# Casting v in its load, state casts and stores on GpSimd, and a new order of steps in an RWKV-5 kernel with a ReLU-squared MLP

## The chip, the cores and the metric

The kernel runs on one core of a Trainium2 chip. The metric is device time in microseconds of one launch, taken as the median of several runs. Engines are named as in the profile: PE is TensorE (PEld its weight loads), DVE is VectorE, ACT is ScalarE, POOL is GpSimd, SP is SyncE. ACTq, POOLq and SPq are the same engines when they issue transfers.

## The reference

For each of 4 batches and 8 heads, with head size 48 and 768 steps, a linear recurrence runs over time; its output, rearranged to 3072 rows of 384, goes through two matrices with a squared ReLU between them.

```python
for t in range(S):
    cur = einsum('bhd,bhe->bhde', u[None] * kt, vt)
    y[:, :, t] = einsum('bhd,bhde->bhe', rt, state + cur)
    state = w[None, :, :, None] * state + einsum('bhd,bhe->bhde', kt, vt)
x = y.transpose(0, 2, 1, 3).reshape(B * S, H * D)
g = maximum(x @ w_in, 0) ** 2          # 384 -> 2048
out = g @ w_out                        # 2048 -> 384
```

All inputs and the output are float32; the kernel multiplies in bf16.

## The kernel before, in words

The time axis is cut into 6 chunks of 128 steps. A *unit* is one chunk of one batch: 24 units, unit i being chunk i // 4 of batch i % 4. For each unit, r and k are loaded and scaled by powers of w (`scale`), turned so that the head dimension lies on the partitions, multiplied (`at`), masked (`mask`), and multiplied with v (`y`), with the state carried from the chunk before; the state is kept in float32 (`st32`) and cast to bf16 (`stb`). The result `yb` is turned (`xT`) and goes through the MLP: `m1` (four pieces for a unit alone, eight for a pair), `relu`, a square on ACT (`sqA`) or DVE (`sqD`), `m2` in four quarters, the eviction `osb` and the store `out`. Units 0 to 5 are handled singly and turned on TensorE; from unit 6 on they go in pairs and are turned by transposing transfers.

Nothing is scheduled by rule: the string `ORDER` names every step, in order, with the PSUM bank it uses behind an `@`, and every engine executes its instructions in that order. A word is step.unit.part. Those that the text below speaks of:

- `kt.i.o`, `rt.i.o`: load half o of k or r of unit i, 96 KB, on SP (line L281); for later units both units of a pair come in one load of 384 KB (L278). `ktA.1.0` is such a half, issued by ACT. `vt.i`: load v on POOL. `I.q`, `O.q`: load quarter q of `w_in` or `w_out` on POOL, cast to bf16 by the load (L288, L291).
- `w.0`, `w.1`: powers of w, an activation each on ACT (L242), from `lnat.0` and `lnat.1` on DVE; `wk`, `wr`: two more on ACT (L245). `scale.i.0` scales r with `w.0`, `scale.i.1` scales k with `w.1`, both on DVE (L303).
- `turn.i.x` turns scaled r (x=0) or k (x=1) on TensorE (L333), `rkT.i.x` evicts it on ACT (L337); `kb.i` and `kbT.i` turn k back. `rk.i` multiplies r and k on DVE (L360), `at.i`, `mask.i.o` (L377), `d.i`, `dv.i`, `y.i`, `yb.i` (L456), `xturn.i`, `xT.i` (L481) lead to the MLP.
- `cols`, `copied`, `uwb`, `end`, `wend`: columns of w and u, turned on TensorE, copied on DVE (`copied`), made into the operands of `d` on POOL (`uwb`), the decay over a chunk on ACT (`end`) and spread out on POOL (`wend`, L268), which the first `sadd` needs.
- `fill.n` are n matmuls of a constant tile (L216) whose result is never read.

Every transfer signals a semaphore. Those issued by SP and ACT share eight (DMAHW0 to 7) and those by POOL another eight (DMASW0 to 7), given out in turn when the program is built. A transfer adds 16 to its semaphore when it has landed, and the engine that issues it first waits until the transfer before it on the same semaphore has landed.

Of the kernel before, what the change touches and what calls it, by code (L numbers as in the profile page):

```python
# [21 lines left out]
scale.2.0 at.1@67 kbT.1 kt.5.0 d.1@3 scale.2.1 m1.0.0@2 vt.5 mask.1.0 rt.5.0 s.1@4 turn.2.0@5 relu.0.0 mask.1.1 O.0
turn.2.1@1 rkT.2.0 fill.2 m1.0.3@6 sadd.1 O.3 rt.5.1 sqA.0.0 dv.1 y.1@0 relu.0.3 scale.3.0 O.1 rt.6 yb.1 stb.1
turn.3.0@2 rkT.2.1 scale.4.0 xturn.1@7 rkT.3.0 sqD.0.3 kt.5.1 kb.2@5 xT.1 at.2@43 rk.2 O.2 kbT.2 turn.4.0@6 mask.2.0
m1.1.2@0 rkT.4.0 kt.6 scale.3.1 d.2@1 vb.3 s.2@2 m1.1.0@7 mask.2.1 relu.1.2 sadd.2 turn.3.1@5 sqA.1.2 m1.0.2@4 dv.2
rkT.3.1 y.2@6 m1.1.3@3 relu.1.0 rk.3 yb.2 relu.0.2 kb.3@0 m1.0.1@2 scale.4.1 sqA.1.0 xturn.2@1 kbT.3 m1.1.1@5
relu.0.1 s.3@7 xT.2 d.3@6 sqD.0.1 at.3@40 relu.1.1 turn.4.1@2 mask.3.1 m1.2.2@1 vb.4 rkT.4.1 dv.3 m1.2.3@5 relu.2.2
mask.3.0 at.4@02 vb.5 rk.4 m2.0.0@6 relu.2.3 mask.4.0 sqA.2.2 m1.2.1@1 sqD.2.3 relu.1.3 m1.2.0@4 mask.4.1 sqA.0.2
sqD.1.3 m2.1.0@5 stb.2 relu.2.0 sadd.3 kb.4@0 y.3@3 relu.2.1 sqD.1.1 y.4@2 stb.3 m2.0.1 yb.3 kbT.4 scale.5.0 m2.1.1
sqA.2.0 sqD.2.1 kt.8 xturn.3@4 s.4@7 xT.3 turn.5.0@1 sadd.4 m2.1.2 rkT.5.0 dv.4 m1.3.1@3 sdec.4 kt.10 yb.4 m1.3.0@0  # L30
stb.4 relu.3.1 scale.6.0 m2.0.2 scale.5.1 relu.3.0 xturn.4@4 scale.7.0 m2.0.3 sqA.3.0 rt.8 sqD.3.1 xT.4 m1.3.3@1
osb.0 scale.6.1 turn.5.1@7 out.0 relu.3.3 m1.4.0@2 scale.7.1 rkT.5.1 m2.3.0@3 sqD.3.3 relu.4.0 rkD.6 m1.4.3@0 rk.5
sqA.4.0 kb.5@4 relu.4.3 at.5@61 m1.4.2@7 kbT.5 mask.5.0 vtS.6 m1.4.1@2 sqD.4.3 relu.4.2 mask.5.1 m2.3.1 sqA.4.2
s.5@0 relu.4.1 y.5@4 dv.5 m2.1.3 sqA.4.1 vtS.8 sadd.5 m1.3.2@6 yb.5 osb.1 sdec.5 out.1 relu.3.2 m2.2.0@7 scale.8.0
stb.5 scale.8.1 m2.2.1 rt.10 sqA.3.2 scale.9.0 m2.2.2 scale.9.1 m2.2.3 m2.3.2 osb.2 rkD.8 rk.6 at.6@1205 xturn.5@4
mask.7.1 m2.4.0@6 xT.5 out.2 mask.6.1 m2.4.1 vb.6 mask.7.0 rt.12 m1.5.3@7 mask.6.0 s.6@5 relu.5.3 s.7@4 dv.6 y.7@2
y.6@0 dv.7 m2.4.2 sqD.5.3 vtS.10 vb.8 m1.5.0@1 yb.6 yb.7 m2.4.3 relu.5.0 sadd.7 xD.6 m1.5.1@7 scale.10.0 sqA.5.0
scale.10.1 m2.3.3 osb.4 relu.5.1 sdec.7 out.4 m1.5.2@0 scale.11.1 osb.3 stb.7 m2.5.0@2 scale.11.0 sqA.5.1 sadd.6
out.3 at.8@1467 relu.5.2 rk.8 rkD.10 m2.5.1 sqA.5.2 mask.8.0 s.8@3 mask.8.1 s.9@5 kt.12 m2.5.2 sdec.6 y.8@0 sadd.8
stb.6 m2.5.3 scale.12.0 mask.9.0 osb.5 sadd.9 out.5 mask.9.1 kt.14 vb.10 m1.6.0@1 sdec.9 dv.8 m1.6.4@4 relu.6.0  # L40
scale.13.0 m1.6.3@2 yb.8 vtS.12 sqA.6.0 sdec.8 m1.6.6@6 relu.6.4 dv.9 relu.6.3 m1.6.7@7 sqA.6.4 sqD.6.3 m1.6.1@3
relu.6.7 rk.10 rt.14 y.9@1 relu.6.6 m1.6.2@0 sqD.6.7 stb.9 relu.6.1 yb.9 at.10@4527 relu.6.2 scale.12.1 s.11@6 xD.8
m1.6.5@3 sqA.6.1 mask.11.1 sqA.6.2 s.10@1 dv.11 m2.6.0@0 vtS.14 relu.6.5 dv.10 m2.6.1 scale.13.1 sqA.6.6 mask.10.0
sqA.6.5 m2.7.0@7 stb.8 rkD.12 mask.11.0 m2.7.1 mask.10.1 m2.7.2 sadd.10 vb.12 m2.6.2 sadd.11 kt.16 sdec.10 m2.6.3
sdec.11 y.10@3 osb.6 y.11@4 stb.10 yb.10 out.6 m2.7.3 stb.11 yb.11 m1.8.0@2 scale.14.0 osb.7 xD.10 scale.14.1
m1.8.1@5 relu.8.0 scale.15.0 m1.8.7@1 scale.15.1 sqA.8.0 out.7 m1.8.3@6 relu.8.1 kt.18 relu.8.7 m1.8.2@0 sqA.8.1
kt.20 sqD.8.7 m1.8.6@3 relu.8.2 m2.8.0@4 relu.8.3 sqA.8.2 m1.8.4@7 sqD.8.3 relu.8.6 at.12@2510 rk.12 relu.8.4 m2.8.1
mask.13.1 sqA.8.6 rkD.14 s.12@6 mask.12.0 sqA.8.4 m1.8.5@3 vb.14 mask.12.1 s.13@7 m1.10.5@0 relu.8.5 sadd.12 rt.16
sadd.13 y.12@2 sqA.8.5 sdec.12 m1.10.6@5 relu.10.5 sdec.13 m2.8.2 stb.12 mask.13.0 sqA.10.5 m1.10.3@3 vtS.16 dv.13
relu.10.6 m1.10.0@0 dv.12 relu.10.3 yb.12 m1.10.1@1 sqA.10.6 sqD.10.3 relu.10.0 y.13@7 vtS.18 m1.10.7@5 relu.10.1  # L50
yb.13 sqA.10.0 m2.8.3 xD.12 relu.10.7 m1.10.4@6 osb.8 sqD.10.7 stb.13 m1.10.2@3 out.8 rk.14 relu.10.4 at.14@2017
vtS.20 relu.10.2 m2.9.0@5 sqA.10.4 mask.14.0 sqA.10.2 s.15@4 mask.15.1 m2.9.1 sqA.10.1 dv.15 rt.18 m2.9.2 sadd.15
m2.11.0@6 mask.15.0 vb.16 sdec.15 m2.11.1 scale.16.0 m2.11.2 scale.16.1 rt.20 m2.11.3 scale.17.0 mask.14.1 s.14@3
osb.11 y.15@2 dv.14 m2.9.3 vb.18 out.11 sadd.14 rt.22 stb.15 y.14@7 scale.17.1 osb.9 m1.12.0@4 sdec.14 out.9
m1.12.7@1 yb.14 stb.14 yb.15 relu.12.0 m1.12.3@0 relu.12.7 rkD.16 m1.12.2@6 sqA.12.0 sqD.12.7 m1.12.1@3 relu.12.3
xD.14 relu.12.2 m1.12.4@5 sqD.12.3 relu.12.1 scale.18.0 m1.12.6@7 sqA.12.2 scale.18.1 m1.12.5@2 sqA.12.1 scale.19.0
m2.10.0@4 relu.12.4 vtS.22 scale.19.1 relu.12.5 scale.20.0 m2.13.0@1 sqA.12.4 scale.20.1 m2.10.1 scale.21.0 sqA.12.5
m2.13.1 scale.21.1 vb.20 rkD.18 m2.10.2 relu.12.6 m2.10.3 sqA.12.6 scale.22.0 m2.13.2 osb.10 scale.23.0 rkD.20
m2.13.3 m2.12.0@0 osb.13 m2.12.1 rk.16 out.13 out.10 at.16@6352 kt.22 s.16@7 mask.17.0 m1.14.5@4 sadd.16 m1.14.1@1
relu.14.5 dv.16 s.17@5 vb.22 mask.16.0 m2.12.2 dv.17 relu.14.1 m1.14.2@4 sadd.17 sqA.14.5 m1.14.7@7 mask.16.1  # L60
sqA.14.1 sdec.17 m1.14.0@6 relu.14.2 sdec.16 relu.14.7 y.16@1 rk.18 sqA.14.2 m1.14.4@5 yb.16 relu.14.0 m2.12.3
sqD.14.7 relu.14.4 m1.14.6@3 osb.12 mask.17.1 sqA.14.4 m1.14.3@4 out.12 rk.20 sqA.14.0 y.17@7 relu.14.3 at.18@1650
yb.17 stb.17 m2.15.0@2 sqD.14.3 xD.16 relu.14.6 mask.18.0 s.21@4 stb.16 m2.14.0@7 sqA.14.6 dv.21 m2.15.1 mask.18.1
s.18@3 mask.19.0 m2.15.2 sadd.18 m2.15.3 dv.18 y.18@1 osb.15 sdec.18 m2.14.1 yb.18 out.15 stb.18 m2.14.2 scale.22.1
mask.19.1 m2.14.3 scale.23.1 s.20@4 s.19@6 osb.14 dv.20 at.20@5321 rkD.22 dv.19 y.19@0 mask.20.0 m1.16.0@7 mask.21.1
out.14 m1.16.2@4 relu.16.0 yb.19 m1.16.1@5 sqA.16.0 mask.21.0 xD.18 m1.16.5@1 relu.16.2 mask.20.1 relu.16.1
m1.16.3@7 sadd.19 relu.16.5 y.21@0 sdec.19 sqA.16.1 m1.16.7@2 stb.19 y.20@4 relu.16.3 m2.16.0@3 yb.20 sqA.16.2
m1.16.6@5 sqD.16.3 relu.16.7 sqA.16.5 yb.21 m1.16.4@6 sqD.16.7 relu.16.6 xD.20 m2.17.0@1 relu.16.4 rk.22 m2.17.1
sqA.16.6 at.22@7420 sqA.16.4 s.22@5 m1.18.4@6 mask.23.0 mask.23.1 m2.17.2 relu.18.4 dv.22 m1.18.6@2 sqA.18.4
mask.22.0 y.23@0 relu.18.6 mask.22.1 m1.18.7@6 sqA.18.6 s.23@5 m1.18.1@7 dv.23 relu.18.7 m1.18.3@2 sqD.18.7  # L70
relu.18.1 m1.18.2@4 sqA.18.1 m1.18.5@5 relu.18.3 relu.18.2 y.22@6 sqD.18.3 m1.18.0@7 relu.18.5 yb.22 sqA.18.2
m2.16.1 yb.23 sqA.18.5 m2.16.2 xD.22 relu.18.0 m2.16.3 sqA.18.0 m2.17.3 osb.16 m1.20.0@2 out.16 osb.17 m2.19.0@4
out.17 relu.20.0 m2.19.1 sqA.20.0 m1.20.4@5 m1.20.7@6 relu.20.4 m2.18.0@0 sqA.20.4 m1.20.1@7 relu.20.7 m1.20.6@3
sqD.20.7 relu.20.1 m2.18.1 sqA.20.1 m2.19.2 relu.20.6 m1.22.2@1 sqA.20.6 m2.19.3 relu.22.2 m1.22.1@2 sqA.22.2
m1.20.2@5 osb.19 relu.22.1 out.19 m1.22.4@6 relu.20.2 m2.20.0@7 sqA.22.1 sqA.20.2 m1.20.3@3 relu.22.4 m2.18.2
# [547 lines left out]
```

## Time and profile before

| | |
|---|---|
| median of 3 runs | 174.9 us (174.62 to 177.03) |
| profiled execution, its time | 173.95 us |
| profiled execution, its span | 172.2 us |
| TensorE clock granted in the profile | 1.00 |
| busy: PE / DVE / ACT / POOL | 165.0 / 121.9 / 131.4 / 15.9 us |
| `fill` matmuls | 104, 10.3 us |
| transfers | 28.86 MB, mean 168 GB/s |

The span is the time between the first and the last event of the program on the core, as the profiler recorded it; the execution's own time is 1.75 us more. Rows of the views in order of time give the start and the length of a run of equal instructions, in microseconds, then engine, line, operation, tiles and count. Rows that group instructions give busy time and the mean of one in nanoseconds, then the idle time just before them and what ended it. Rows of transfers give the issuing engine, the count, the size and the median time from issue to landing.

### The profile page before, as it was taken

The numbers are of one execution on the slowest core, as the hardware profiler recorded it, in microseconds if no ns is written. First come the engines' busy times: TensorE is split into PE (matmuls) and PEld (weight loads), VectorE is DVE, ScalarE is ACT, GpSimd is POOL, SyncE is SP. The second block draws the span as 40 slices with busy tenths as digits, with TensorE's granted clock in tenths as the row PEclk, the third lists the DMA queues.
The fourth block names the chain that finished last, engine by engine and source line by source line (L and its number), as shares of the span: only waits on it lengthen the run. The fifth ranks groups of instructions, "written<-read, shape, count | busy, mean of one in ns | idle before, by whom it ended". The sixth has DMA issues, their size and how long they took to land.

```text
span 172.2 us, 4759 instructions
## 1 busy us (share of the span) xinstructions
PE 165.0 (96%) x1964; PEld 135.8 (79%) x1964; DVE 121.9 (71%) x243; ACT 131.4 (76%) x255; POOL 15.9 (9%) x36
## 2 busy tenths in 40 slices
...
GB/s 95 180 289 235 277 235 216 209 197 243 154 247 222 247 194 236 203 173 251 168 227 230 186 201 245 165 239 212 46 213 50 0 25 116 0 46 49 0 127 58
DMA packets 91493, 28.86 MB, mean 168 GB/s; under 512 B 82864, under 2 KB 90672, under 8 KB 91472
## 3 DMA queue, kind: packets, MB, share of 16 engines
...
q0 software_dynamic: 2624, 4.33, 12.4%
q10 hardware_dynamic: 432, 0.25, 0.6%
...
q14 instruction: 6, 0.05, 0.1%
...
## 4 chain that ended last, share of the span: by engine, by line
PE 81%; DMA 8%; DVE 4%; ACT 2%; SPq 2%; issue 1%; DVEq 0%
PE bank L517 34%; PE bank L493 31%; DMA rkT<-rkw 5%; DMA rt<-in_r_dram 4%; PE bank L369 3%; PE bank L441 2%; PE bank L398 2%; PE bank L447 2%; SPq L281 2%; PE bank L533 2%; PE bank L410 1%; PE bank L333 1%; PE bank L216 1%; DVE rkw L303 1%; DVE am L377 1%
## 5 line engine op out<-in xcount | busy, mean ns | idle before, releaser
L493 PE MATMUL bank<-xT,w_in_q 128*128 128x256 bf16 (+1 forms) x720 | 72.1, 251 | 0.0
L517 PE MATMUL bank<-w_out_q,g 128*128 128x384 bf16 x368 | 67.6, 326 | 0.0
L493 PEld LDWEIGHTS <-w_in_q 128*128 128x128 bf16 x720 | 64.0, 113 | 3.3
L501 ACT ACTIVATE gr<-bank 128x512 f32<-128x512 f32 x96 | 55.1, 603 | 10.0 <-PE bank L493 9.8
L517 PEld LDWEIGHTS <-g 128*128 128x128 bf16 x368 | 34.3, 98 | 18.3
L508 ACT ACTIVATE g<-gr 128x512 bf16<-128x512 f32 x68 | 42.0, 640 | 0.8
L510 DVE TENSOR_TENSOR g<-gr 128x512 bf16<-128x512 f32 x28 | 19.3, 688 | 24.1 <-ACT gr L501 23.9
L377 DVE TENSOR_TENSOR am<-bank,smask 128x512 bf16<-128x512 f32 x48 | 31.5, 683 | 3.8 <-PE bank L369 3.7
L524 ACT COPY osb<-bank 128x384 f32<-128x384 f32 x23 | 11.0, 479 | 10.7 <-PE bank L517 10.6
L456 DVE TENSOR_TENSOR yb<-bank,dv 128x384 bf16<-128x384 f32 x24 | 12.9, 551 | 1.0 <-PE bank L447 0.8
L420 DVE TENSOR_TENSOR dv<-vb,bank 128x384 f32<-128x384 bf16 x24 | 12.8, 547 | 0.9 <-PE bank L398 0.5
L432 ACT CAST stb<-st 128x384 bf16<-128x384 f32 x20 | 10.4, 523 | 3.1 <-DVE st L428 3.0
L216 PE MATMUL bank<-warm 128*128 128x128 bf16 x104 | 10.3, 269 | 1.1 <-DVE warm L161 1.1
L301 DVE TENSOR_TENSOR rkw<-rt,wpos 128x384 bf16<-128x384 f32 x18 | 9.8, 551 | 0.8 <-DMA rt<-in_r_dram 0.8
L316 ACT CAST vb<-vt 128x768 bf16<-128x768 f32 x9 | 7.6, 841 | 3.4 <-DMA vt<-in_v_dram 3.4
L301 DVE TENSOR_TENSOR rkw<-kt,wneg 128x384 bf16<-128x384 f32 x18 | 9.8, 550 | 0.0
L216 PEld LDWEIGHTS <-warm 128*128 128x128 bf16 x104 | 8.7, 124 | 1.2 <-DVE warm L161 1.0
L369 PE MATMUL bank<-rkT 64*128 64x128 bf16 x192 | 8.0, 219 | 0.9 <-DMA rkT<-rkw 0.9
L424 DVE TENSOR_TENSOR st<-bank,st 128x384 f32<-128x384 f32 x16 | 8.6, 550 | 0.2 <-PE bank L398 0.2
L441 PE MATMUL bank<-vb,am 128*128 128x48 bf16 x192 | 8.7, 183 | 0.0
L357 DVE TENSOR_TENSOR rk<-rkT 128x1024 bf16<-128x1024 bf16 x9 | 6.2, 686 | 3.4 <-DMA rkT<-rkw 3.4
L428 DVE TENSOR_TENSOR st<-st,wend 128x384 f32<-128x384 f32 x16 | 8.6, 551 | 0.0
...
## 6 DMA issues: line engine op xcount, KB each, us to landing
...
rt<-in_r_dram SPq DMA_DIRECT2D x9, 384.0 KB, 4.8
kt<-in_k_dram SPq DMA_DIRECT2D x9, 384.0 KB, 4.8
vt<-in_v_dram SPq DMA_DIRECT2D x9, 384.0 KB, 5.3
w_in_q<-in_moe_w_in_dram POOLq DMA_DIRECT2D x4, 384.0 KB, 8.2
w_out_q<-in_moe_w_out_dram POOLq DMA_DIRECT2D x4, 384.0 KB, 13.0
...
kt<-in_k_dram SPq DMA_DIRECT2D x11, 96.0 KB, 7.6
```

Source lines behind the costliest of these rows:

```text
L216: nc.tensor.matmul(out=banks[0][:, :128], lhsT=warm, rhs=warm, start=True, stop=True)
L301: nc.vector.tensor_tensor(t["rkw"][:, x, :, :, :D], pair(src), pair(wneg if x else wpos), ALU.mult)
L369: nc.tensor.matmul(out=t["at"][o][:, p, :], lhsT=t["rkT"][sl, 1, p, :], rhs=t["rkT"][sl, 0, p, :], start=True, stop=True,)
L377: nc.vector.tensor_tensor(am, t["at"][o], smask.unsqueeze(1).to_broadcast([C, HP, C]), ALU.mult)
L420: nc.vector.tensor_tensor(t["dv"], t["vb"], t["d"].unsqueeze(2).to_broadcast([C, H, D]), ALU.mult)
L441: nc.tensor.matmul(out=y[:, 2 * p + o, :], lhsT=t[f"am{o}"][:, p, :], rhs=t["vb"][:, 2 * p + o, :], start=(o == 0 and p == 0), stop=c == 0 ...
L456: nc.vector.tensor_tensor(t["yb"], t["y"], t["dv"].rearrange("p h d -> p (h d)"), ALU.add)
L493: nc.tensor.matmul(out=t["h", s][:, a], lhsT=turned, rhs=chunks[c]["xT"][:, b : b + m, n, :], start=(n == 0), stop=(n == NK - 1),)
L501: nc.scalar.activation(t["gr", s], t["h", s], AF.Relu)
L508: nc.scalar.activation(g, x, AF.Square)
L510: nc.vector.tensor_tensor(g, x, x, ALU.mult)
L517: nc.tensor.matmul(out=t["o"], lhsT=chunks[units[i][0]]["g"][:, f, units[i][1], :], rhs=w_out_q[f // 4][:, f % 4, :], start=(f == 0), stop ...
```

## The change

- v of units 0 to 5 is loaded by POOL straight into the bf16 tile `vb`; the cast on ACT (`vb.0` to `vb.5`) goes.
- The first state cast of each batch (`stbP.0` to `stbP.3`) is a copy on POOL instead of ACT.
- The stores of units 0 to 21 (`outP`) are issued by POOL instead of SP; those of units 22 and 23 stay on SP.
- The string `ORDER` is another one: order, banks and the number of fills (57 in place of 104).

```diff
 ORDER = """
-kt.0.0 kt.0.1 rt.0.0 rt.1.0 I.0 rt.1.1 ids fill.25 log@4567 ktA.1.0 lnat.0 rt.2.0 vt.0 lnat.1 w.0 fill.1 cols@1
-kt.1.1 w.1 upper copied kt.2.0 end scale.0.0 wk kt.2.1 vt.1 scale.0.1 wr fill.14 turn.0.0@2 rt.2.1 turn.0.1@3 zeros
-rkT.0.0 rt.3.0 vt.2 rkT.0.1 scale.1.0 rt.3.1 uwb fill.16 at.0@14 rk.0 kb.0@5 mask.0.1 turn.1.0@6 I.3 kbT.0 rt.4.0
-mask.0.0 fill.4 d.0@7 rkT.1.0 I.2 vb.0 vb.1 rt.4.1 dv.0 wend fill.17 s.0@2 y.0@3 scale.1.1 kt.3.0 vb.2 vt.3 yb.0
...
-sqD.22.3 m2.20.3 m1.22.6@0 osb.20 m2.21.3 out.20 relu.22.6 m2.22.0@1 sqA.22.6 m2.22.1 osb.21 out.21 m2.22.2 m2.22.3
-m2.23.0@4 osb.22 out.22 m2.23.1@5 osb.23.0 out.23.0 osb.23.1 out.23.1
+rt.0.0 kt.0.0 kt.0.1 rt.1.0 I.3 rt.1.1 ids lnat.0 fill.17 log@4567 kt.1.1 vt.0 w.0 lnat.1 cols@3 ktA.1.0 rt.2.0
+scale.0.0 upper w.1 rt.2.1 fill.3 turn.0.0@2 vt.1 scale.0.1 kt.2.0 rkT.0.0 copied kt.2.1 wk I.0 fill.5 turn.0.1@2 wr
+I.2 rt.3.0 rkT.0.1 vt.2 rk.0 fill.6 at.0@16 scale.1.0 rt.3.1 kb.0@7 zeros mask.0.0 turn.1.0@2 uwb kt.3.0 mask.0.1
+rkT.1.0 kbT.0 scale.1.1 fill.10 y.0@3 d.0@2 kt.3.1 turn.1.1@7 dv.0 s.0@4 rkT.1.1 rt.4.0 yb.0 end rk.1 fill.8 kb.1@1
+rt.4.1 wend xturn.0@5 at.1@76 scale.2.0 xT.0 kbT.1 rt.5.0 mask.1.0 I.1 fill.7 turn.2.0@3 mask.1.1 d.1@2 rkT.2.0 O.0
+fill.1 m1.0.0@7 kt.4.0 scale.2.1 vt.3 sadd.0 y.1@5 turn.2.1@1 dv.1 kt.4.1 rkT.2.1 stbP.0 yb.1 relu.0.0 m1.0.3@2 vt.4
+rk.2 rt.5.1 scale.3.0 at.2@31 relu.0.3 kb.2@4 O.1 mask.2.1 kt.5.0 xturn.1@5 d.2@7 kbT.2 m1.0.2@0 xT.1 dv.2
+turn.3.0@6 kt.5.1 relu.0.2 mask.2.0 m1.1.3@4 sqA.0.0 scale.3.1 y.2@3 rkT.3.0 m1.1.0@1 rt.6 yb.2 turn.3.1@5 relu.1.0
+s.1@7 kt.6 xturn.2@3 s.2@0 sadd.1 rkT.3.1 m1.1.2@6 sadd.2 stbP.1 relu.1.3 m1.0.1@2 scale.4.0 O.3 relu.1.2 sqD.0.3
...
+sqA.22.5 relu.22.0 m1.22.3@0 relu.22.7 m2.19.3 sqA.22.2 m2.21.1 sqA.22.0 m2.21.2 relu.22.3 osb.19 sqD.22.3 m2.22.0@3
+outP.19 sqD.22.7 m2.21.3 m2.20.2 osb.21 m2.20.3 m2.22.1 osb.20 m2.22.2 outP.20 outP.16 m2.23.0@4 outP.18 outP.21
+outP.17 m2.22.3 m2.23.1@2 osb.23.1 osb.22 osb.23.0 out.22 out.23.1 out.23.0
 """
...
     def load_v(i):
         c, b = units[i]
-        whole = of_two("vt", i, loads, [C, H, D], F32)
         if i >= NH:
+            whole = of_two("vt", i, loads, [C, H, D], F32)
             nc.sync.dma_start(out=whole.rearrange("s b h d -> s (b h) d"), in_=both(v, i))
         else:
-            nc.gpsimd.dma_start(out=tiles[i]["vt"], in_=v[b, :, c * C : (c + 1) * C, :].rearrange("h s d -> s h d"))
+            of_two("vb", i, work, [C, H, D])
+            nc.gpsimd.dma_start(out=tiles[i]["vb"], in_=v[b, :, c * C : (c + 1) * C, :].rearrange("h s d -> s h d"))
...
-    def state_cast(i):
+    def state_cast(i, copy=nc.scalar.copy):
         b = units[i][1]
-        nc.scalar.copy(stb[b], st32[b])
+        copy(stb[b], st32[b])
...
-    def store(i):
+    def store(i, queue=nc.sync):
         c, b = units[i]
-        nc.sync.dma_start(out=out[b * S + c * C : b * S + (c + 1) * C, :], in_=tiles[i]["osb"])
+        queue.dma_start(out=out[b * S + c * C : b * S + (c + 1) * C, :], in_=tiles[i]["osb"])
```

The first instructions of ScalarE in the two built programs, with the semaphores that they wait for and the count (W), and the semaphore of each load (U):

```
before                                        changed
load wrow            U DMAHW0                 load wrow            U DMAHW0
load rt.0.1          U DMAHW2                 load rt.0.1          U DMAHW2
lnw                  W DMAHW0 16              lnw                  W DMAHW0 16
load ktA.1.0         U DMAHW7                 w.0                  W DVE 17
w.0                  W DVE 17                 load ktA.1.0         W DMAHW1 48, U DMAHW1
w.1                  W DVE 18                 w.1                  W DVE 18
```

In the changed program the loads on DMAHW1 ahead of `ktA.1.0` are `rt.0.0`, `rt.2.1` and `rt.4.1`, SP's 1st, 8th and 16th; `rt.2.1` waits for `rt.0.0`, and `rt.4.1` for `rt.2.1`. On POOL, in both, the loads of each semaphore follow each other in the order of the list.

More of the change, by code (lines that the diff above doesn't have):

```diff
@@ L22 @@
[L22 to L75, printed above, removed]
-relu.20.3 m2.18.3 sqA.22.4 sqD.20.3 m1.20.5@1 osb.18 m1.22.5@4 out.18 relu.20.5 m2.21.0@2 sqA.20.5 m2.21.1 relu.22.5
@@ new lines @@
+turn.3.0@6 kt.5.1 relu.0.2 mask.2.0 m1.1.3@4 sqA.0.0 scale.3.1 y.2@3 rkT.3.0 m1.1.0@1 rt.6 yb.2 turn.3.1@5 relu.1.0
+s.1@7 kt.6 xturn.2@3 s.2@0 sadd.1 rkT.3.1 m1.1.2@6 sadd.2 stbP.1 relu.1.3 m1.0.1@2 scale.4.0 O.3 relu.1.2 sqD.0.3
+kb.3@7 xT.2 at.3@01 O.2 sqA.0.2 rk.3 turn.4.0@4 mask.3.0 m1.1.1@3 sqA.1.0 mask.3.1 d.3@6 kbT.3 m1.2.1@5 relu.1.1
+scale.4.1 y.3@0 rkT.4.0 dv.3 m1.2.3@7 relu.2.1 yb.3 turn.4.1@1 relu.0.1 m1.2.0@4 sqD.1.3 rkT.4.1 m2.1.0@3 scale.5.0
+relu.2.3 sqD.1.1 m1.2.2@2 relu.2.0 sqD.0.1 at.4@75 kb.4@6 mask.4.0 turn.5.0@4 kbT.4 s.3@1 m2.0.0@0 mask.4.1 rkT.5.0
@@ new lines @@
+xturn.3@6 rk.4 m2.1.1 xT.3 sqD.2.1 sqA.1.2 s.4@5 y.4@7 dv.4 relu.2.2 m2.0.1 rt.8 sadd.3 m1.3.1@4 scale.5.1 stbP.3
+sadd.4 m2.1.2 stbP.2 relu.3.1 yb.4 vt.5 m1.3.3@1 vtS.6 sqA.2.0 scale.6.0 turn.5.1@5 m1.3.0@7 rkT.5.1 scale.7.0
+xturn.4@2 m2.0.2 xT.4 sqA.2.2 m2.0.3 scale.6.1 kt.8 relu.3.0 m2.1.3 scale.7.1 sqD.2.3 at.5@75 osb.1 kb.5@4 mask.5.1
+m1.4.0@2 kbT.5 rkD.6 rk.5 relu.3.3 m2.2.0@6 mask.5.0 relu.4.0 m2.2.1 sqD.3.3 s.5@2 scale.8.0 m1.3.2@1 sadd.5 rt.10
+m1.4.3@4 sdec.5 vb.6 dv.5 y.5@3 m2.2.2 sqD.3.1 relu.4.3 vtS.8 osb.0 m2.2.3 scale.9.0 sqA.4.0 scale.8.1 m1.4.2@7
@@ new lines @@
+sqA.3.0 yb.5 m1.4.1@5 relu.3.2 scale.9.1 kt.10 osb.2 sqD.4.3 m2.3.0@0 relu.4.2 rk.6 xturn.5@1 relu.4.1 m2.3.1 xT.5
+at.6@4276 sqA.4.2 rkD.8 m2.4.0@3 sqA.4.1 mask.6.0 sqA.3.2 s.6@5 mask.7.1 s.7@1 m1.5.3@4 sadd.7 mask.7.0 m2.4.1
+relu.5.3 mask.6.1 m2.4.2 stb.5 vtS.10 dv.6 y.7@6 dv.7 y.6@4 rt.12 m1.5.0@2 yb.6 m2.4.3 yb.7 relu.5.0 scale.10.0 xD.6
+m1.5.1@1 osb.4 sadd.6 sqA.5.0 m1.5.2@6 scale.10.1 relu.5.1 scale.11.0 m2.3.2 kt.12 relu.5.2 scale.11.1 m2.5.0@2
+sqA.5.1 sdec.4 at.8@5613 vb.8 sqD.5.3 m2.3.3 rk.8 sqA.5.2 rkD.10 vb.10 mask.8.1 m2.5.1 stb.4 mask.8.0 s.9@7 osb.3
```

49 lines of the change are left out of this document (41 added, 8 removed).

## The prediction

> **What bounds the kernel now.** I read the page first, for the shares, then busy time by stretches, then the first 16 us in order of time, then the loads' times to landing.
>
> ```profile
> span 172.2 us, 4759 instructions
> PE 165.0 (96%) x1964; PEld 135.8 (79%) x1964; DVE 121.9 (71%) x243; ACT 131.4 (76%) x255; POOL 15.9 (9%) x36
> ...
> L216 PE MATMUL bank<-warm 128*128 128x128 bf16 x104 | 10.3, 269 | 1.1 <-DVE warm L161 1.1
> ```
>
> ```profile
> 16.00:20.00 4.00, 3.15 (x58) 2.61 (x56) 4.00 (x9) 3.85 (x9) 1.31 (x3) 1.00 1.17 253
> 20.00:24.00 4.00, 4.00 (x82) 4.00 (x81) 3.94 (x9) 3.97 (x9) 0.00 (x0) 1.00 1.13 270
> ...
> 64.00:68.00 4.00, 3.84 (x56) 2.89 (x53) 4.00 (x8) 4.00 (x9) 0.00 (x0) 1.00 1.01 220
> ...
> 88.00:92.00 4.00, 3.06 (x39) 2.07 (x39) 3.04 (x6) 2.23 (x5) 0.00 (x0) 1.00 1.12 217
> ```
>
> The columns are PE, PEld, DVE, ACT and POOL busy, with counts in brackets. From 16 us to its end TensorE idles only 0.85, 0.16 and 0.94 us in the three stretches that are not full, 1.95 in all. So the end is set by when TensorE's dense work begins, plus a fixed amount of matmuls, plus the tail. The dense work begins at the first `m1`, line L493; the tail is the last store.
>
> ```profile
> 15.27 0.84 PE L493 MATMUL bank<-xT,w_in_q 128*128 128x128 bf16 x12
> ...
> 165.93 2.80 PE L533 MATMUL bank<-w_out_q,g 128*128 128x256 bf16 x32
> 168.28 1.15 SPq L549 DMA_DIRECT2D out_dram<-osb  x2
> 168.77 0.29 DVE L545 COPY osb<-bank 128x128 f32<-128x128 f32 x1 [7.17 <-PE bank L533]
> ```
>
> TensorE ends at 165.93 + 2.80 = 168.73. From `m1.0.0` that is 153.46 us, of which 1.95 are idle and about 0.1 two fills: the matmuls are 151.4. The tail is 172.2 - 168.73 = 3.5.
>
> **The part that decides: one load on ScalarE's queue.** Before:
>
> ```profile
> 3.30 0.54 ACTq L281 DMA_DIRECT2D kt<-in_k_dram  x1
> 3.34 0.28 ACT L190 ACTIVATE lnw<-wrow 128x96 f32<-128x96 f32 x1
> 4.25 1.11 ACT L242 ACTIVATE wfour<-lnat 128x384 f32<-128x384 f32 x2 [0.63 <-DVE lnat L237]
> ...
> 10.21 0.56 DVE L303 TENSOR_TENSOR rkw<-rt,wfour 128x384 bf16<-128x384 f32 x1 [3.75 <-DMA rt<-in_r_dram]
> ```
>
> `ktA.1.0` (half of k of unit 1) goes out at 3.30 without a wait. In the changed program it stands between `w.0` and `w.1`, and its semaphore is DMAHW1, on which it is the fourth load, after `rt.0.0`, `rt.2.1` and `rt.4.1`; it waits for 48, which is when `rt.4.1` has landed. Behind it on ScalarE stand `w.1` and every eviction; `scale.0.1` on VectorE needs `w.1`, `scale.1.1` needs this very load. Nothing on SP's list up to `rt.4.1` needs ScalarE, so it ends, but late. That such waits hold their queue, the trace shows on SP and on GpSimd:
>
> ```profile
> 12.14 1.18 SPq L281 DMA_DIRECT2D kt<-in_k_dram  x2
> kt<-in_k_dram SPq DMA_DIRECT2D x1, 96.0 KB, 7.6
> 19.78 10.82 SPq L281 DMA_DIRECT2D kt<-in_k_dram  x1
> POOL w_out_q L291 <- DMA w_in_q<-in_moe_w_in_dram: 2.6, 2, 2.3
> ```
>
> `kt.3.0` goes out at 12.14 and lands 7.6 later, at 19.74; `kt.5.1`, next on the same semaphore, starts at 19.78. No row shows it on ScalarE. The Trainium skill, "DMA: Bandwidth & Descriptors", section "Anatomy of one DMA", states that DMA engines do not wait on semaphores, and that the wait is on the issuing sequencer; by that rule ScalarE's own list stands still, as I take it.
>
> When does `rt.4.1` land? It is SP's 16th load, and waits for `rt.2.1`, SP's 8th. The first eight go out as before, since their semaphores are free early:
>
> ```profile
> 5.78 1.06 SPq L281 DMA_DIRECT2D kt<-in_k_dram  x1
> kt<-in_k_dram SPq DMA_DIRECT2D x1, 96.0 KB, 6.9
> 7.54 4.43 SPq L281 DMA_DIRECT2D rt<-in_r_dram  x5
> rt<-in_r_dram SPq DMA_DIRECT2D x1, 96.0 KB, 6.2
> ...
> rt<-in_r_dram SPq DMA_DIRECT2D x1, 96.0 KB, 5.2
> ...
> kt<-in_k_dram SPq DMA_DIRECT2D x1, 96.0 KB, 7.9
> ```
>
> The 8th goes out at 5.78 and lands 6.9 later, at 12.7. The 16th then goes out, and takes between 5.2 (a load issued near 9) and 7.9 (issued at 12.72, beside weights and v on GpSimd's queue). In the change GpSimd stops after `vt.2`, since its next step needs `cols`, copied behind `scale.0.1`; so I take the 6.2 of a load issued at 7.54. T, the moment when ScalarE goes on, is 12.7 + 6.2 = 18.9 (17.9 to 20.6).
>
> **From T to the first m1.** The durations:
>
> ```profile
> L242 ACT ACTIVATE wfour<-lnat 128x384 f32<-128x384 f32 x2 | 1.0, 522 | 0.7 <-DVE lnat L237 0.6
> L337 ACT COPY rkT<-bank 128x512 bf16<-128x512 bf16 x12 | 6.9, 593 | 1.0 <-PE bank L333 1.0
> L303 DVE TENSOR_TENSOR rkw<-kt,wfour 128x384 bf16<-128x384 f32 x6 | 3.3, 551 | 0.0
> L377 DVE TENSOR_TENSOR am<-bank,smask 128x512 bf16<-128x512 f32 x48 | 31.5, 683 | 3.8 <-PE bank L369 3.7
> L456 DVE TENSOR_TENSOR yb<-bank,dv 128x384 bf16<-128x384 f32 x24 | 12.9, 551 | 1.0 <-PE bank L447 0.8
> L481 ACT COPY xT<-bank 128x384 bf16<-128x384 bf16 x6 | 2.9, 489 | 1.3 <-PE bank L477 1.3
> kt<-in_k_dram ACTq DMA_DIRECT2D x1, 96.0 KB, 5.5
> 1.05 2.58 PEld L216 LDWEIGHTS <-warm 128*128 128x128 bf16 x25 [1.05 <-DVE warm L161]
> 11.36 0.96 PEld L216 LDWEIGHTS <-warm 128*128 128x128 bf16 x17
> ```
>
> Times after T: the issue 0.54, `w.1` to 1.06. ScalarE then does `rkT.0.0`, `wk`, `wr` and `rkT.0.1`, starting about 0.5 apart: to 3.2; `scale.0.1` and `turn.0.1` lie beside this. VectorE: `rk.0` and `scale.1.0` to 4.2, two masks to 5.4, `scale.1.1` from 5.5, when the load has landed (5.5), to 6.05. TensorE: after `kb.0` and `turn.1.0` ten fills, `y.0`, `d.0`, to 6.85; then `dv.0` and `yb.0` (0.55 each) to 7.95; `xturn.0` behind eight fills and `kb.1`, to 9.2; `xT.0` 0.49, to 9.7; `at.1`, seven fills and `turn.2.0` mostly beside it. `m1.0.0` starts at about T + 10. Bounds: before, 9.91 passed from the end of `w.1` (5.36) to `m1.0.0`, 3.75 of them VectorE's wait for a load; so T + 7.2 to T + 11.0.
>
> A fill in this walk costs 0.10, as the first 25 do (2.58/25); seventeen at 11.36 take 0.056 each. With the quick ones `m1.0.0` is about a microsecond earlier. The Trainium skill, "TensorE: Matmul & The Clock Gate", Part 1, states that TensorE's clock halves after some 3.4 us of idleness, until it was as long busy; here it idles from about 7 to T + 1.7. By that rule the slow pace is right, and up to 1.7 us of the first `m1` are lost on top (an estimate from the page's figure). The sum leaves this out.
>
> `m1.0.0` at 18.9 + 10 = 28.9.
>
> **After it.** Matmuls 151.4, less `turn.2.0` (0.2), already done: 151.2. GpSimd resumes only with ScalarE, so weights come late:
>
> ```profile
> DMA to landing us min/median/max: 6.9/8.2/10.4
> w_out_q<-in_moe_w_out_dram POOLq DMA_DIRECT2D x1, 384.0 KB, 11.2
> ...
> w_out_q<-in_moe_w_out_dram POOLq DMA_DIRECT2D x1, 384.0 KB, 14.1
> L268 POOL COPY wend<-wend_c 64x192 f32<-64x192 f32 x2 | 0.7, 339 | 0.1
> ```
>
> The first row is that of `w_in_q`. `I.1` follows `wend` (0.7), which follows `end` behind `rkT.1.1`: out at T + 9.1, landed at T + 17.3. `m1.0.1` is due 6.4 us of matmuls after `m1.0.0`, at T + 16.4: a wait of 0.9 (0 to 3.1). `O.2` stands behind `stbP.1`, which needs `s.1` (T + 15.5): out at T + 17.3, landed at T + 28.5 to 31.4, and `m2.1.2` is due at T + 28.3: I take 1.6. Of the later idle time of before I keep 0.16 + 0.94. Waits: 3.6 in all.
>
> TensorE ends at 28.9 + 151.2 + 3.6 = 183.7.
>
> **The tail.** Now `m2.22.3` and `m2.23.1` come last, and SP issues `out.22`, `out.23.1`, then the larger half `out.23.0`, which was issued first before.
>
> ```profile
> out_dram<-osb SPq DMA_DIRECT2D x1, 128.0 KB, 2.8
> ...
> out_dram<-osb SPq DMA_DIRECT2D x1, 64.0 KB, 2.1
> ```
>
> One more issue (0.3 to 0.6) ahead of the last store, and 2.8 in place of 2.1 to land: +0.9, so 4.4 (3.5 to 4.8). GpSimd's last five stores, 0.56 to 0.9 each behind `osb.20` (some 4.1 us ahead of TensorE's end), are issued by then and land inside it.
>
> **The other parts, beside the path.**
>
> ```profile
> L318 ACT CAST vb<-vt 128x384 bf16<-128x384 f32 x6 | 3.1, 520 | 0.6 <-DMA vt<-in_v_dram 0.5
> L432 ACT CAST stb<-st 128x384 bf16<-128x384 f32 x20 | 10.4, 523 | 3.1 <-DVE st L428 3.0
> SPq L553 <- ACT osb L524: 25.2, 8, 7.9
> L291 POOL DMA_DIRECT2D w_out_q<-in_moe_w_out_dram x4 | 2.2, 556 | 2.6 <-DMA w_in_q<-in_moe_w_in_dram 2.6
> ```
>
> ScalarE loses six casts of v and four of states, 3.1 + 2.1 us: worth at most the 0.85 that TensorE idled in 16 to 20 us, already taken off. A cast on GpSimd costs between 0.52 (ScalarE's) and 0.68 (two of `wend`'s copies); I take the latter, nearer as the same engine's. 22 stores cost GpSimd some 0.56 each; it is idle then, so nothing is behind them; if it were not, `stbP` and the late weights would be. SP's 25.2 us of waits for `osb` go; its transposes can start earlier, but TensorE waited 0.9 us for them in all. 47 fewer fills remove no work: they stood where TensorE had to wait.
>
> **The sum.** 183.7 + 4.4 = 188.1 of span, 15.9 over 172.2. The profiled execution took 173.95, 0.95 under the median of 174.9; from the median the forecast is 174.9 + 15.9 = 190.8.
>
> **The rivals.** *The wait is not met late (not slower).* If the load went out as soon as ScalarE reaches it, at 4.8, say because the chip runs it under a free semaphore as it did before, it lands by 10.3 to 11.7 (5.5 to 6.9), `scale.1.1` follows, and `m1.0.0` comes 4.5 after that, at about 15.5: 15.5 + 151.2 + 2.5 + 4.4 = 173.6 of span, 176.3 on the median, within 2%. It decides as long as the load is out by 6.9 (2% is 3.5 us). The unhindered ScalarE load of before speaks for it, the fixed count of 48 against it. A ScalarE that runs past the wait would not do: VectorE still stands at `scale.1.1` until T + 5.5, and `m1.0.0` comes at T + 10.
>
> *Slower still.* `ktA.1.0`, once out, lands like the slowest load of its size.
>
> ```profile
> DMA to landing us min/median/max: 2.8/6.6/14.5
> ```
>
> With 14.5 in place of 5.5 all moves 9 on: 199.8. It needs large loads in flight beside it; SP's 384 KB loads of units 6 and 7 go out just then. Against it: GpSimd's weights, in flight when the 14.5 was seen, are held back here.
>
> **Chances and range.** Forecast 0.84, load not held 0.06, slower still 0.10. With the low ends (T -1.0, walk -2.8, waits -2.5, tail -0.9) it is 183.6; with the high ones (T +1.7, walk +1.0, waits +3.7, tail +0.4) 197.6. Range 184 to 198. A change under 2% can hardly be told from none: faster 0.02, same 0.05, slower 0.93.
>
> **What would show it.** ScalarE idle from about 5 to 19 us with one `kt` issue on its queue, ended by an `rt` load; VectorE idle as long; TensorE's share near 87%; `m1.0.0` near 29; dense matmuls and a tail near 4.4 after that. I am wrong if `kt` leaves ScalarE's queue before 10 us, or if the lost time lies behind 40 us.

## The result, and the profile after

The changed kernel takes 185.03 us (median of 6 runs, 183.96 to 185.88), the kernel before 175.14 on the same chip (6 runs, 173.22 to 177.03): ratio 1.0586, 95% interval 1.0519 to 1.0653, so it is slower, by some 10 us. The forecast was 190.8, the range 184 to 198: the time lies in the range, 1 us above its low end, and the loss was forecast at 15.9 us where it is 9.9. The experiments ran on other chips, whose kernel before took 177.85 to 178.08; so they are compared by ratios, each to the kernel before on its own chip. Ratios come from undisturbed runs, and taking all runs instead moves a ratio by up to 1.1%: no difference under that is claimed.

The head of the page of the changed kernel:

```profile
span 183.0 us, 4673 instructions
PE 162.6 (89%) x1917; PEld 132.9 (73%) x1917; DVE 122.4 (67%) x243; ACT 125.5 (69%) x245; POOL 29.6 (16%) x62
```

The span is 10.8 us longer, and TensorE is busy 2.4 us less. The instructions of the changed kernel in order of time, from the first scaling on:

```profile
5.10 0.56 DVE L303 TENSOR_TENSOR rkw<-rt,wfour 128x384 bf16<-128x384 f32 x1
...
10.83 1.25 SPq L281 DMA_DIRECT2D rt<-in_r_dram  x2
...
18.07 0.54 ACTq L281 DMA_DIRECT2D kt<-in_k_dram  x1
18.66 0.52 ACT L242 ACTIVATE wfour<-lnat 128x384 f32<-128x384 f32 x1 [13.60 <-DMA rt<-in_r_dram]
19.22 0.56 DVE L303 TENSOR_TENSOR rkw<-kt,wfour 128x384 bf16<-128x384 f32 x1 [13.56 <-DMA kt<-in_k_dram]
...
23.13 0.55 DVE L303 TENSOR_TENSOR rkw<-kt,wfour 128x384 bf16<-128x384 f32 x1
...
27.15 0.84 PE L491 MATMUL bank<-xT,w_in_q 128*128 128x128 bf16 x12
```

The fourth row is `w.1`: ScalarE stood idle for 13.60 us ahead of it, until a load of r had landed, and its own load `ktA.1.0` left only at 18.07, in the row above. VectorE's `scale.0.1` (the fifth row) waited as long for `w.1`; the releaser that the row names, a load of k, had long landed, and the instruction that really came last is the one that ends just ahead of it. `m1.0.0` starts at 27.15, 11.88 later than before. Busy time by stretches, PE, PEld, DVE, ACT and POOL:

```profile
8.00:20.00 12.00, 0.17 (x2) 0.17 (x3) 0.63 (x2) 1.34 (x3) 1.90 (x5) 1.00 1.40 230
27.15:178.95 151.80, 150.84 (x1783) 123.03 (x1783) 112.03 (x211) 118.11 (x230) 18.91 (x34) 1.00 0.78 147
```

In the first stretch almost nothing runs on any engine. From `m1.0.0` to TensorE's end at 178.95 it idles 151.80 - 150.84 = 0.96 us in all. Of the waits below the first is that of ScalarE for the semaphore of `ktA.1.0`; the other two are TensorE's in that stretch:

```profile
ACT wfour L242 <- DMA rt<-in_r_dram: 13.6, 1, 13.6
...
PE bank L491 <- DVE dv L418: 0.5, 1, 0.5
PE bank L491 <- DMA xT<-yb: 0.4, 1, 0.4
```

The tail, in order of time:

```profile
177.89 1.06 PE L531 MATMUL bank<-w_out_q,g 128*128 128x128 bf16 x16
...
179.31 0.85 SPq L547 DMA_DIRECT2D out_dram<-osb  x2
```

From 178.95 to the end of the span are 4.05 us. So the whole loss is in the first 27 us: +11.88 for `m1.0.0`, -1.66 between it and TensorE's end, +0.6 for the tail.

### The profile page after: what moved, and what is told of

Its sections match the earlier page's. It is cut to its first block, busy times and chain, and to the rows that moved or that the text cites. A ratio compares the mean times of both kernels' runs of the same rounds, so it can differ in the third digit from the quotient of the medians.

```text
span 183.0 us, 4673 instructions
## 1 busy us (share of the span) xinstructions
PE 162.6 (89%) x1917; PEld 132.9 (73%) x1917; DVE 122.4 (67%) x243; ACT 125.5 (69%) x245; POOL 29.6 (16%) x62
## 4 chain that ended last, share of the span: by engine, by line
PE 82%; DMA 9%; SPq 2%; DVE 2%; ACT 2%; issue 0%; ACTq 0%
PE bank L491 34%; PE bank L515 32%; DMA rt<-in_r_dram 7%; PE bank L367 4%; PE bank L439 3%; DMA xT<-yb 3%; SPq L281 2%; PE bank L445 2%; PE bank L396 2%; PE bank L531 1%; PE bank L331 1%; PE bank L343 1%; PE bank L216 1%; ACT rkT L335 1%; PE bank L408 1%; PE bank L475 1%
## 5 line engine op out<-in xcount | busy, mean ns | idle before, releaser
L515 PE MATMUL bank<-w_out_q,g 128*128 128x384 bf16 x368 | 68.8, 326 | 0.0
L506 ACT ACTIVATE g<-gr 128x512 bf16<-128x512 f32 x68 | 40.7, 632 | 0.2
L551 POOL DMA_DIRECT2D out_dram<-osb x22 | 11.8, 542 | 119.3 <-ACT osb L522 119.1
L331 PE MATMUL bank<-identb,rkw 128*128 128x128 bf16 x48 | 5.5, 249 | 13.0 <-DVE rkw L303 13.0
L331 PEld LDWEIGHTS <-rkw 128*128 128x128 bf16 x48 | 3.5, 109 | 13.6 <-DVE rkw L303 13.2
L303 DVE TENSOR_TENSOR rkw<-kt,wfour 128x384 bf16<-128x384 f32 x6 | 3.3, 549 | 13.6 <-DMA kt<-in_k_dram 13.6
L242 ACT ACTIVATE wfour<-lnat 128x384 f32<-128x384 f32 x2 | 1.0, 523 | 14.2 <-DMA rt<-in_r_dram 13.6
L335 ACT COPY rkT<-bank 128x512 bf16<-128x512 bf16 x12 | 7.1, 594 | 4.2 <-PE bank L331 4.2
```

The lines of the kernel that those rows point to most:

```text
L506: nc.scalar.activation(g, x, AF.Square)
L515: nc.tensor.matmul(out=t["o"], lhsT=chunks[units[i][0]]["g"][:, f, units[i][1], :], rhs=w_out_q[f // 4][:, f % 4, :], start=(f == 0), stop ...
L551: queue.dma_start(out=out[b * S + c * C : b * S + (c + 1) * C, :], in_=tiles[i]["osb"])
```

## The experiments

The theory: one word of `ORDER` does it, since `ktA.1.0` shares a semaphore with `rt.4.1` where it now stands. The rivals: that ScalarE's queue, and not the late data, is what costs; and that another part of the change costs too.

**The load ahead of `w.0` again (e1_early).** The changed kernel with one word moved; the load then waits for nothing.

```diff
-... lnat.0 fill.17 log@4567 kt.1.1 vt.0 w.0 lnat.1 cols@3 ktA.1.0 rt.2.0
+... lnat.0 fill.17 log@4567 ktA.1.0 kt.1.1 vt.0 w.0 lnat.1 cols@3 rt.2.0
```

> The changed kernel, with ktA.1.0 moved ahead of w.0 (behind log), where it gets the free semaphore DMAHW7 and waits for nothing. Theory 1 (the load's wait is the whole loss): ScalarE never stands still for 13.6 us, the load goes out by 4.2 and lands by about 9.5, m1.0.0 starts at 14 to 16 instead of 27.1, and all that follows keeps its 151.8 us and its tail of 4.0: span 170 to 172, ratio to before 0.98 to 1.00. Theory 2 (weights, v and stores on GpSimd's queue, or the new order itself, cost some of it): m1.0.0 as early, but idle time of TensorE behind it grows; span 175 or more.

Measured: 180.83 us, ratio 1.017 (1.012 to 1.0221), span 179.5. Instructions in order of time, then waits, then busy time by stretches:

```profile
16.71 0.83 PE L491 MATMUL bank<-xT,w_in_q 128*128 128x128 bf16 x12
...
19.82 5.87 SPq L278 DMA_DIRECT2D kt<-in_k_dram  x1
25.80 6.44 SPq L278 DMA_DIRECT2D rt<-in_r_dram  x1
```

```profile
PE bank L491 <- DMA xT<-yb: 2.9, 1, 2.9
```

```profile
84.00:88.00 4.00, 1.36 (x14) 1.17 (x15) 0.93 (x2) 1.05 (x3) 0.00 (x0) 0.87 1.25 196
88.00:92.00 4.00, 4.00 (x37) 2.99 (x35) 3.09 (x6) 2.06 (x4) 0.00 (x0) 0.70 0.96 202
...
16.71:175.57 158.86, 153.28 (x1784) 123.64 (x1783) 112.30 (x211) 118.78 (x230) 18.56 (x33) 0.99 0.83 156
```

The wait is gone and `m1.0.0` comes 10.44 us sooner, as the theory has it (at 16.71, a little behind the 14 to 16 expected). But the gain is smaller: by the ratios 4.2%, some 7 us, and the profiled spans, which are of two chips, differ by 3.5 only. After `m1.0.0` TensorE now idles 5.58 us in place of 0.96, 2.9 of them for one transposing transfer; SP, which issues it, spends 5.87 and 6.44 us on two loads from 19.82 us on; and the matmuls take 153.28 in place of 150.84, with the granted clock at 0.87 and 0.70 around that wait. The long issues on SP are no sign by themselves: the kernel before has one of 10.82 us (at 19.78, shown in the prediction). So the wait is the larger part, and something else in the change costs 1.7% that the standstill had covered.

**The same load on SP (e2_sp).** The changed kernel with `kt.1.0` in the place of `ktA.1.0`, so that SP issues it as its 7th.

> The changed kernel, with the same load issued by SP as its 7th (kt.1.0) instead of by ScalarE; all of SP's later loads come one place later. Theory 1: no standstill; the load goes out near 4.7, lands near 11, m1.0.0 at 15 to 17: span 171 to 174, ratio 0.985 to 1.01, at most 2 us above the kernel with the load on ScalarE ahead of w.0. Theory 2: span 175 or more.

Measured: median 180.89 (176.44 to 183.35), too scattered for a ratio. Its profile has the same wait for `xT`, 3.0 us. On the loss it decides nothing beside e1_early. On the clock it does: the same two stretches, with an idle time as long, show 1.00 in the column of the granted clock (third from the end).

```profile
84.00:88.00 4.00, 1.02 (x9) 0.61 (x7) 1.71 (x4) 1.66 (x4) 0.00 (x0) 1.00 1.23 218
88.00:92.00 4.00, 4.00 (x52) 3.73 (x50) 3.12 (x6) 2.51 (x5) 0.00 (x0) 1.00 0.98 196
```

**The wait alone, in the kernel before (e3_before_late).** Only the place of one word changes.

```diff
-... rt.1.1 ids fill.25 log@4567 ktA.1.0 lnat.0 rt.2.0 vt.0 lnat.1 w.0 fill.1 cols@1
+... rt.1.1 ids fill.25 log@4567 lnat.0 rt.2.0 vt.0 lnat.1 w.0 ktA.1.0 fill.1 cols@1
```

> The kernel before, with one word moved: ktA.1.0 stands between w.0 and w.1 instead of ahead of them. It then waits on DMAHW0 for 48, the landing of kt.3.0, SP's 15th load. Nothing else of the change is in it. Theory 1: ScalarE stands still from about 5 to 17 to 19.5, m1.0.0 starts 9 to 10 later, at 26 to 29.5, span 182 to 186, ratio 1.055 to 1.08. Theory 2 (this kernel's loss comes with the change's other parts): ratio below 1.02.

Measured: 186.45 us, ratio 1.0466 (1.0365 to 1.0568). A wait, then an instruction in order of time:

```profile
ACT wfour L242 <- DMA kt<-in_k_dram: 12.1, 1, 12.1
```

```profile
25.82 0.84 PE L493 MATMUL bank<-xT,w_in_q 128*128 128x128 bf16 x12
```

Here the load falls on another semaphore, whose last load ahead of it is `kt.3.0`; it waits for that one, and `m1.0.0` moves from 15.27 to 25.82. One word, with no other part of the change, makes the kernel slower by nearly as much as the whole change.

**ScalarE free, the data late (e4_act_free).** In the changed kernel the load goes behind `kbT.0`, so that `w.1` and all that ScalarE does up to `kbT.0` pass it.

```diff
-... vt.0 w.0 lnat.1 cols@3 ktA.1.0 rt.2.0
+... vt.0 w.0 lnat.1 cols@3 rt.2.0
...
-rkT.1.0 kbT.0 scale.1.1 fill.10 ...
+rkT.1.0 kbT.0 ktA.1.0 scale.1.1 fill.10 ...
```

> The changed kernel, with ktA.1.0 moved behind kbT.0 on ScalarE, so that w.1 and the evictions of unit 0 go on; the load still waits, on DMAHW3 for 48, the landing of kt.4.0, SP's 18th load. Theory 1a (the late data is enough: VectorE stands at scale.1.1): m1.0.0 at 26 to 30, span 181 to 186, ratio 1.04 to 1.08. Theory 1b (it is ScalarE's standstill that costs, because w.1 and every eviction are behind it): the work of unit 0 is out of the way, m1.0.0 no later than 22, span under 178.

Measured: 185.71 us, ratio 1.0465 (1.0396 to 1.0534), span 183.6. Instructions in order of time, then a wait:

```profile
4.27 1.12 ACT L242 ACTIVATE wfour<-lnat 128x384 f32<-128x384 f32 x2 [0.63 <-DVE lnat L237]
...
27.99 0.83 PE L491 MATMUL bank<-xT,w_in_q 128*128 128x128 bf16 x12
```

```profile
DVE rkw L303 <- DMA kt<-in_k_dram: 12.1, 1, 12.1
```

`w.1` runs at once, and little or nothing is won by it (1.0465 against 1.0586, with intervals that overlap): VectorE stands at `scale.1.1` for 12.1 us instead, since the load is as late, and ScalarE's standing still is not the point. That is what the prediction said of a ScalarE that runs past the wait.

**v as float32 again, without the wait (e5_vf32, then f2_vf32_again).** e1_early with the loads and casts of v of units 0 to 5 as they were before the change.

```diff
-nc.gpsimd.dma_start(out=tiles[i]["vb"], in_=v[b, :, c * C : (c + 1) * C, :]...)
+nc.gpsimd.dma_start(out=tiles[i]["vt"], in_=v[b, :, c * C : (c + 1) * C, :]...)
...
+            nc.scalar.copy(tiles[i]["vb"], tiles[i]["vt"])
```

> The kernel with ktA.1.0 ahead of w.0, and with v of units 0 to 5 loaded in float32 and cast by ScalarE again, as before the change; stores and first state casts stay on GpSimd, the order stays. Theory 1 (the casting loads, 6144 packets of 96 bytes, take some 7.5 us of the sixteen transfer engines' time while these are full, and all later loads and transposes come late by that): GpSimd's queue falls from 64% to about 47% of the first 45 us, the 2.9 us that TensorE waits for xT near 84 us go or shrink below 1, ratio to before 0.985 to 1.005. Theory 2 (SP's new order, or the stores on GpSimd, make the transposes late): the wait near 84 us stays within a microsecond, ratio 1.01 to 1.03.

> The same kernel as e5_vf32, beside the next one on one chip, to see whether its lead over the kernel before stands. If it does: ratio 0.983 to 0.995. If it was the chip or a few runs: 0.995 to 1.005.

Measured: ratio 0.989 (0.9838 to 0.9942), and on a second chip 1.0026 (0.9935 to 1.0116). A lead over the kernel before isn't shown; that the 1.7% of e1_early are gone is. GpSimd's queue in the first 45 us, of e1_early and then of e5_vf32 (packets, MB, share of 16 engines' time), and TensorE's wait for `xT` in e5_vf32, 2.9 us in e1_early:

```profile
q0 software_dynamic: 8480, 3.74, 64.1%
```

```profile
q0 software_dynamic: 2624, 4.33, 47.5%
```

```profile
PE bank L493 <- DMA xT<-yb: 0.7, 1, 0.7
```

Both are as the first theory has them. This version still has the new order, its fills, the stores and the state casts on GpSimd: together they cost nothing that shows.

**v cast by its load, in the kernel before (b_vcast).** The same part alone, in the other kernel: the loads of the change, and `vb.0` to `vb.5` taken out of the order.

> The kernel before, with one part of the change: v of units 0 to 5 cast to bf16 by its load, and ScalarE's six casts dropped; order else as before. Theory 1: 7.5 us more of transfer time in the first 45 us; loads of units 3 to 5 and the weights land later, TensorE waits 1 to 4 us more before 40 us or for transposes near 90 us; ratio 1.005 to 1.03. Theory 2: transfers have enough slack, and ScalarE's 3.1 us help: ratio 0.98 to 1.00.

Measured: 180.35 us, ratio 1.0136 (1.0081 to 1.019). Transfers in the first 45 us, of the kernel before and then of this one; a queue's row has packets, MB and the share of 16 engines' time:

```profile
q0 software_dynamic: 2624, 4.33, 47.4%
...
w_out_q<-in_moe_w_out_dram POOLq DMA_DIRECT2D x4, 384.0 KB, 13.0
vt<-in_v_dram POOLq DMA_DIRECT2D x6, 192.0 KB, 7.3
```

```profile
q0 software_dynamic: 8480, 3.74, 63.6%
...
w_out_q<-in_moe_w_out_dram POOLq DMA_DIRECT2D x4, 384.0 KB, 18.2
...
vb<-in_v_dram POOLq DMA_DIRECT2D x6, 96.0 KB, 10.4
```

GpSimd's queue moves 0.59 MB less in 5856 packets more, and takes 16.2% more of the 45 us, which is 7.3 us of all 16 engines. The load lands later although it counts half the bytes, and so do the weights behind it. TensorE waits for them, where in the kernel before the only transfer that it waited for was `rkT`, 0.9 us:

```profile
PE bank L515 <- DMA w_out_q<-in_moe_w_out_dram: 2.3, 1, 2.3
PE bank L367 <- DMA rkT<-rkw: 1.5, 2, 1.2
PE bank L491 <- DMA w_in_q<-in_moe_w_in_dram: 1.3, 2, 0.9
```

The Trainium skill, "DMA: Bandwidth & Descriptors", section "Specifications", puts the least transfer for full rate at 512 B. A row of 48 values is 96 B in bf16, which is under that. It is 192 B in float32, but the float32 load doesn't move by such rows. That is seen where the two forms stand beside the same other loads, in the changed kernel and in f1_wait_vf32 (below), each with five loads of v in its first 45 us:

```profile
DMA packets 21364, 8.08 MB, mean 179 GB/s; under 512 B 16240, under 2 KB 20848, under 8 KB 21360
```

```profile
DMA packets 16485, 8.57 MB, mean 191 GB/s; under 512 B 11120, under 2 KB 15728, under 8 KB 16480
```

The casting loads make 5120 packets under 512 B more, 1024 for each load, which is one for each row of 128 steps and 8 heads; so the float32 loads make none that short. The trace agrees with the figure in kind: fewer bytes in short packets took longer.

**v as float32, the wait kept (f1_wait_vf32).** The same edit as in e5_vf32, in the changed kernel itself.

> The changed kernel, wait of ktA.1.0 kept, but v of units 0 to 5 loaded as float32 and cast on ScalarE as before. Theory 1 (the lost time is the standstill, and while it lasts the transfers get ahead, so that the small packets of the casting load cost nothing here): T stays near 18 us, span 181.5 to 184, ratio to the kernel before 1.045 to 1.06, no lower than the changed kernel by more than 0.7%. Theory 2 (the casting load costs its 1 to 3% here too, beside the standstill): ratio 1.015 to 1.04.

Measured: ratio 1.0579 (1.0518 to 1.064), span 186.3; in order of time:

```profile
19.74 0.59 ACTq L281 DMA_DIRECT2D kt<-in_k_dram  x1
...
29.42 0.83 PE L493 MATMUL bank<-xT,w_in_q 128*128 128x128 bf16 x12
```

The ratio is that of the changed kernel (1.0586), as the first theory has it. The span was expected at 184 at most and was 186.3, since the wait ended at 19.74 and not near 18. Why it ended later isn't shown. From the end of the wait to the end of the span it took 166.6 us, the changed kernel, on another chip, 164.9: behind the standstill too the float32 load won nothing. So the four cases are:

| ratio to the kernel before | v cast by its load | v cast on ScalarE |
|---|---|---|
| the wait kept | 1.0586 | 1.0579 |
| the wait taken away | 1.017 | 0.989 and 1.003 |

The two costs don't add: the casting load costs 1.4 to 2.8% where TensorE starts early, and nothing that shows behind the standstill.

**The stores (e6_sp_stores, b_stores, f3_stores_again).** e6_sp_stores is e1_early with every `outP` as `out`, on SP; b_stores is the kernel before with its stores 0 to 21 and its first state casts on GpSimd.

> The kernel with ktA.1.0 ahead of w.0, and with all stores issued by SP at the places of the new order; v still cast by its loads. Theory 1: the transposes come no earlier, since the transfer engines are as full; SP has 22 issues more, so ratio to before 1.015 to 1.03. Theory 2, in its form that stores on GpSimd collide with the transposes: the wait near 84 us goes, ratio 0.99 to 1.005.

> The kernel before, with two parts of the change: the first state cast of each batch and the stores of units 0 to 21 on GpSimd; order else as before. Both theories of the loss leave this near no change, since GpSimd is idle after 20 us and SP's transposes no longer stand behind osb: ratio 0.985 to 1.005. A third theory (GpSimd's stores are slow for every transfer beside them): ratio above 1.01.

> The same kernel as b_stores (the kernel before, with only its stores 0 to 21 and its first state casts on GpSimd). Its first runs scattered from 173.94 to 177.66, and the ratio of 0.983 rested on the three lowest. If the move of the stores is worth something by itself: ratio 0.975 to 0.99 again. If not, as the prediction priced it: 0.993 to 1.003.

Measured: e6_sp_stores 1.0099 (1.0059 to 1.014), which overlaps the interval of e1_early (1.012 to 1.0221) and lies in neither theory's range; TensorE still waits 2.0 us for `xT` there, so the stores on GpSimd are not what makes that wait; b_stores 0.9828 (0.9741 to 0.9914), and on a second chip 0.9909 (0.9847 to 0.997). The second of these lies between the two ranges that were expected, and under the 1.1% below which nothing is claimed. So whether the two moves are worth anything in the kernel before stays open, and in the new order they were not seen to gain.

## Why the prediction was right, and where its numbers were off

**The mechanism held step by step.** ScalarE stopped at the one load, until `rt.4.1`; VectorE stood as long; TensorE's share is 89% (87 forecast); the loss lies ahead of 28 us. e3_before_late shows it by itself, e4_act_free that the late data is enough. The sizes were worse than the mechanism: every term of the sum was too long. Against the spans the sum was 5.1 us too long (188.1 and 183.0): T 0.83, the walk 0.92, the matmuls 0.36, the waits 2.64, the tail 0.35. The tail's own terms, 0.3 to 0.6 and 0.7, make 1.0 to 1.3 and not the 0.9 that was added; it grew by 0.58, as the store of 128 KB landed in 1.9 us and not in 2.8. The forecast added 0.95 from the profiled run to the median; it was 0.27. That makes up the 5.8 us.

**T was nearly right by luck, since two errors cancel.** It was put at 18.9 and was 18.07. `rt.4.1` left at 10.83, earlier than 12.7: the 8th load, `rt.2.1`, went out at 5.31 and landed in 5.2 us, where 5.78 and 6.9 were taken. But `rt.4.1` took 7.2 to land and not 6.2. Loads issued between 10 and 12.1 us, and the loads of the whole run:

```profile
rt<-in_r_dram SPq DMA_DIRECT2D x3, 96.0 KB, 7.2
```

```profile
kt<-in_k_dram ACTq DMA_DIRECT2D x1, 96.0 KB, 4.7
...
w_in_q<-in_moe_w_in_dram POOLq DMA_DIRECT2D x4, 384.0 KB, 7.3
w_out_q<-in_moe_w_out_dram POOLq DMA_DIRECT2D x4, 384.0 KB, 7.0
```

**The walk was T + 9.08, not T + 10.** The load landed in 4.7 us, not 5.5, and far from the 14.5 of the rival "slower still". `scale.1.1` started at T + 5.06, when VectorE was done with its masks. The rest took 4.02 against 4.5 forecast.

**The mis-sized term: the waits, 0.96 for 3.6.** They were costed by weights that land in 8.2 and 11.2 to 14.1 us, as before. They landed in 7.3 and 7.0 us, and TensorE waited for none. The same program without the standstill, e1_early, in its first 45 us:

```profile
w_in_q<-in_moe_w_in_dram POOLq DMA_DIRECT2D x4, 384.0 KB, 8.2
w_out_q<-in_moe_w_out_dram POOLq DMA_DIRECT2D x4, 384.0 KB, 10.2
```

So of the 6 us by which `w_out_q` landed sooner than in the kernel before (13.0), some 3 come with the standstill (e3_before_late, the kernel before with a standstill alone, has 9.9), and the rest with the other parts of the change. SP's loads went ahead in the standstill; that it is their lead which made room for the weights is likely, and not shown. The prediction held GpSimd back and did not ask what that lead is worth.

**The parts priced at nothing.** The casting load was priced by ScalarE's 3.1 us alone, with no cost as a transfer. That doesn't show in the total, because the standstill covers it (f1_wait_vf32); by itself it costs 1.4% (b_vcast). The rival "the wait is not met late" said 176.3; with the wait really gone the changed kernel took 1.017 times the kernel before (e1_early), 1.7% over it and not 0.8. The casting load was missing there too, and the rival's 2.5 us of waits, for which no working is shown, were 5.58 in e1_early. The stores on GpSimd were priced at nothing as well, and no run shows otherwise.

**The half clock.** The prediction set aside up to 1.7 us that the first `m1` might lose. Matmuls of the changed kernel in order of time:

```profile
19.83 0.61 PE L331 MATMUL bank<-identb,rkw 128*128 128x128 bf16 x4 [12.97 <-DVE rkw L303]
21.68 0.61 PE L343 MATMUL bank<-identb,rkT 128*128 128x128 bf16 x4
25.30 0.40 PE L343 MATMUL bank<-identb,rkT 128*128 128x128 bf16 x4
26.53 0.39 PE L331 MATMUL bank<-identb,rkw 128*128 128x128 bf16 x4
```

After 13 us of idleness four matmuls take 0.61, five us later 0.39 to 0.40, and `m1.0.0` took 0.84 at 27.15, as it did before. The Trainium skill, "TensorE: Matmul & The Clock Gate", Part 1, has the clock low after idleness and up again after some 3.4 us of work; the trace agrees in kind, with 13 us of idleness and quick matmuls at 25.30, five us after work began again. It cost the first `m1` nothing, since the walk ahead of it was work enough. The column of the granted clock showed 1.00 through all of this.
